# Six score bursts instead of five, six PSUM banks in strict turns, later stores and a reordered first chunk in a transformer block on one Trainium2 core

## The chip, the cores and the metric

The kernel runs as one program on one core of a Trainium2 chip. The metric is the device time of one execution in microseconds (us); smaller is better. A core has a matmul engine (TensorE, PE in the profile, with its weight loads on a row of their own, PEld), a vector engine (VectorE, DVE), an engine for activations (ScalarE, ACT), GpSimd (POOL) and a queue that only issues DMAs (SyncE, SP). Each engine runs its own instructions in the order of the program and waits on semaphores for the others.

## The reference

One input x of 2048 x 640 is normalised, and goes through an attention branch with a sliding window of 256 keys and through a gated feed-forward branch; both are added to x.

```python
def _A_ref(x, wqkv, wo):
    B, S, D = x.shape
    H = 32; Dh = D // H; W = 256
    qkv = (lambda x, *d: x.transpose(*d))((x @ wqkv).reshape(B, S, 3, H, Dh), 2, 0, 3, 1, 4)
    q, k, v = qkv[0], qkv[1], qkv[2]
    scores = jnp.einsum("bhqd,bhkd->bhqk", q, k) * (Dh ** -0.5)
    idx = jnp.arange(S)
    mask = (idx[:, None] - idx[None, :] >= 0) & (idx[:, None] - idx[None, :] < W)
    scores = jnp.where(mask[None, None], scores, -1e9)
    p = _softmax(scores, axis=-1)
    o = jnp.einsum("bhqk,bhkd->bhqd", p, v)
    return (lambda x, *d: x.transpose(*d))(o, 0, 2, 1, 3).reshape(B, S, D) @ wo

def _B_ref(x, w_gate, w_up, w_down):          # 640 -> 1728 -> 640
    g = jnp.einsum("bsd,df->bsf", x, w_gate)
    u = jnp.einsum("bsd,df->bsf", x, w_up)
    h = _gelu(g) * u
    return jnp.einsum("bsf,fd->bsd", h, w_down)

xn = _layernorm(x, axis=-1)
return x + _A_ref(xn, A_wqkv, A_wo) + _B_ref(xn, B_w_gate, B_w_up, B_w_down)
```

All tensors are float32.

## The kernel before, in words

**Precision.** A float32 product is made of three matmuls in a rounded format: the high part of one side by the high and the low part of the other, and low by high. The high part of a tile is a ScalarE copy (`xh`, `wqh`, `wvh`), the low part a subtraction on VectorE or GpSimd (`xl`, `wql`, `wvl`). A "dense group" (line 110) is 15 such matmuls (three times five pieces of 128 input features) into one PSUM tile of 512 tokens, `ps_d`, or of 320 v columns, `ps_v`.

**Chunks.** The 2048 tokens are four chunks of 512, each of four x tiles of 128 rows. A chunk is loaded (`ln_load`), normalised (`ln_stats`, `ln_sqrt`, `ln_rstd`; `ln_apply` is line 164, which scales the tile in place), turned by PE transposes through PSUM (`turn`, line 181, tiles `ps_t`) and split into xh and xl. The first chunk has a function of its own, `first_chunk`, whose order on PE, ScalarE, VectorE and GpSimd is written out by hand: x tiles 0 and 1 are the left half, tiles 2 and 3 the right half; `high(k)` (line 352) and `low(k)` (line 349) split one of five turned pieces; `high_qk` (line 361) and `low_qk` (line 366) split the weights of q (`w0`) and k (`w5`), and `part` is five matmuls of a half. A one-column GpSimd copy from an x tile (lines 378 and 397) serves only to hold the engine until that tile is scaled. `load_v` is a generator: its first step loads the v weights, five more split them (lines 301 and 302), and at its end `v_tiles` fills the v tiles' constant columns (lines 312 and 313). Outside the hand-written parts a scheduler at build time sets the order, so the fills of `ones` (lines 441 and 442, which eight DMAs then spread over the k tiles, line 445) and of `mask` (from line 467) stand wherever it finds a place on GpSimd.

**q and k.** `save_qk` takes a finished dense group of q or k apart into three bfloat16 layers of `pt` (two buffers): `upper` on ScalarE (line 277), `middle` on VectorE into the single buffer `r` (line 273), `lower` on ScalarE (line 258) and GpSimd (line 259), and `store`, DMAs by SP to DRAM (line 268). `load_stack` loads them back by SP in another layout (`ks<-kd`, `qs<-qd`, line 493).

**Attention.** There are 32 units (8 groups of four heads times four chunks), each of 14 slots. `defer(n, fn)` puts a step n slots later. In each slot PE gets what the hand-written order says and then dense matmuls as filler (`pull_fill`, 34.05 matmuls per unit). Three kinds of work use the ring of six PSUM banks, by `bank(name)`:

- `ps_m` (line 522), raw scores of which VectorE takes the row maximum (line 526, `mx`): four tiles in slot 0, four more behind the output in slot 0, four each in slots 4 and 8;
- `ps_e` (line 581), scores with the maximum folded in, of which ScalarE takes the exponential (line 583, `P`); a unit has twelve, and `SCORES` says in which slot each is made;
- `ps_o` (line 608), the product of the previous unit's P with v, copied out by ScalarE (`ob`, line 612); and `ps_n`, a small transpose of the maxima.

That makes 30 tiles a unit. GpSimd clears the masked corners of P (lines 594 and 597). `x_sums` makes sums of x tiles on GpSimd (`tx`, line 739) and stores them by SP (`td<-tx`, line 743).

`load_stack(u + 3)` stands in slot 9 of unit u for k and in slot 12 for q, so that SP's order is fixed by slots too.

**After attention** come the remaining gate and up products (line 952, 570 to 800 us), and then, in steps of `steps`, the down and output projections (line 1219). There each pass over 256 tokens has ten steps; a step n also prepares weights for later passes, as the table `plan` says. An operation `p20` stands for piece 0 of weight set t2, one ScalarE copy (line 1419) and one VectorE subtraction of the high part; `f` fetches, `h` and `l` split a whole set. At the end of a pass VectorE adds eight PSUM banks into the result (`drain`, with `u` and `m` as its scratch tiles).

Of the kernel before, what the change touches and what calls it, by code (L numbers as in the profile page):

```python
# [19 lines left out]
C = 512  # L20
# [11 lines left out]
BURSTS = 0, 4, 8  # L32
SCORES = {0: range(0, 1), 2: range(1, 5), 4: range(5, 7), 8: range(7, 9), 10: range(9, 12)}
RATE = 34.05
# [36 lines left out]
def block_kernel(ctx, tc, x, wqk, wv, wgu, wdo, wdl, out):  # L71
# [76 lines left out]
    def ln_sqrt(mv, n, lp):  # L148
        ve = lp.tile([128, n], F32, name="ve", tag="ve", bufs=2)
        sq = lp.tile([128, n], F32, name="sq", tag="sq", bufs=2)  # L150
        nc.vector.tensor_tensor(out=ve, in0=mv[:, :, 1], in1=eps[:, 0:n], op=OP.add)
        nc.scalar.activation(sq, mv[:, :, 1], AF.Sqrt, bias=eps[:, 0:1])
        return ve, sq
# [75 lines left out]
    def defer(n, fn, *a):  # L229
        if now[0] is None:  # L230
            fn(*a)
        else:
            at(now[0] + n, fn, *a)
# [17 lines left out]
    def save_qk(t, c, ps):  # L251
# [5 lines left out]
        def lower():  # L257
            nc.scalar.activation(pt[:, 1, :], r, AF.Copy)  # L258
            nc.gpsimd.tensor_tensor(out=pt[:, l, :], in0=r, in1=pt[:, 1, :], op=OP.subtract)  # L259
            defer(2, store)  # L260

# [71 lines left out]
    def run(*gens):  # L333
        for gen in gens:
            for _ in gen:
                pass
# [7 lines left out]

    def first_chunk(xs, wr0, wr5, lp):
        halves = slice(0, 256), slice(256, 512)
# [4 lines left out]
        def high(k, ps, cs):  # L351
            nc.scalar.activation(xh[:, k, cs], ps, AF.Copy)
# [6 lines left out]
        def high_qk(raw):  # L359
            wh = wp.tile([128, KT, 128], F32R, name="wqh", tag="wqh")  # L360
            nc.scalar.activation(wh, raw, AF.Copy)
            return wh
# [6 lines left out]
        with tc.manual_schedule(engines=MANUAL | {mybir.EngineType.Pool}):  # L369
# [13 lines left out]
            high(0, ta[0], halves[0])  # L383
            for k in range(1, 4):
                high(k, ta[k], halves[0])
            wh5 = high_qk(wr5)
            vb = ln_sqrt(mv[1], 2, lp)
            high(4, ta[4], halves[0])
            for k in range(2):
                low(k, ta[k], halves[0])  # L390
            rs = ln_rstd(*vb, 2, lp)
# [5 lines left out]
            nc.gpsimd.tensor_copy(one[:, 0:1], xs[3][:, 0:1])  # L397
            w5 = low_qk(wr5, wh5)
            tb = [turn(0, xs[2:4], "o")]
            for k in range(2, KT):  # L400
                low(k, ta[k], halves[0])
# [22 lines left out]
    with tc.tile_pool(name="lp", bufs=1, side="right") as lp:  # L424
# [11 lines left out]
        xs += [ln_load(t, lp) for t in range(4, 8)]  # L436
        w0, w5, mv1 = first_chunk(xs, wr0, wr5, lp)
        run(prep)
        v0 = v0[0]
        ones = lp.tile([4, 2 * C], BF, name="ones")  # L440
        nc.gpsimd.memset(ones, 0.0)
        nc.gpsimd.memset(ones[0:2], 1.0)
# [37 lines left out]
    pf.close()  # L480
    psr = pp.enter_context(tc.tile_pool(name="psr", bufs=6, space=PSUM, reuse_waits="tile"))
    ap = pr.enter_context(tc.tile_pool(name="ap", bufs=2, side="right", reuse_waits="tile"))

    def load_stack(u, which=(0, 1)):
# [4 lines left out]
        for i in which:  # L489
            dst, src, top, again = ((qs[u % NQ], qd[c], 1, 2), (ks[u % NK], kd[c], 0, 0))[i]  # L490
            for j in (0, 2):
                for p, part, n in ((j * 32, top, 2), (j * 32 + 2 * DH, again, 1), (64 - j * 32, 0, 3)):
                    nc.sync.dma_start(dst[p:p + DH * n, j:j + 2].rearrange("p j t -> p (j t)"),
                                      src[g, part:part + n].rearrange("s (d j) t -> (s d) (j t)",
                                                                      j=4)[:, j * C:(j + 2) * C])

    def bank(name):
        return psr.tile([128, C], F32, name=name, tag="ring")

# [228 lines left out]
    def x_sums(p, k, half):  # L728
# [12 lines left out]
        def store(i):  # L741
            t = live[i]
            defer(4, lambda: nc.sync.dma_start(td[p][i][:, k, half * w:half * w + w], t))

# [593 lines left out]
    for j, f in enumerate(range(NFA, NF - 1)):  # L1338
# [50 lines left out]
        if not end:  # L1389
# [14 lines left out]
            7: "ft6 ft8 hb8 lb8", 8: "ft7 ht6 lt6", 9: "ft0 ht8", 10: "lt8 ht7 lt7", 11: "ft1 ft2 ht0 lt0",  # L1404
            12: "ft3 ht1 lt1", 15: "p20", 17: "p21", 21: "p22", 22: "p23", 23: "p30", 24: "p31", 25: "p32", 26: "p33"}

# [101 lines left out]
```

## Time and profile before

| what | us |
|---|---|
| runs | 1047.75, 1049.51, 1049.57 |
| median | 1049.51 |
| the profiled execution's own time | 1048.57 |
| its span, first to last instruction | 1046.8 |
| PE busy in it | 1035.2 |
| VectorE, ScalarE, GpSimd busy | 730.8, 513.5, 333.8 |

The profile is that of one execution. Time of the profiled execution and span differ by what lies before the first and after the last instruction. In rows of the timeline the first column is the start, the second how long the instructions of the row lasted from the first start to the last end, then engine, line, operation, out<-in, and the count. What stands in square brackets is the engine's idle time ahead of the row and what ended it. In rows of waits the three numbers are the total, the number of waits and the longest. Ends of matmuls are modelled.

### The profile page before, as it was taken

How to read it: one execution, taken by the hardware profiler on the slowest of the kernel's cores; microseconds unless marked ns; L12 is line 12 of the kernel's file. 1: busy time of each engine (PE TensorE's matmuls, PEld its weight loads, DVE VectorE, ACT ScalarE, POOL GpSimd, SP SyncE). 2: the span in 40 equal slices, each digit the busy share in tenths (PEclk: the TensorE clock that was granted, in tenths of full speed). 3: DMA queues.
4: the chain of work that ended last, by engine and by line, in shares of the span. 5: the costliest groups of instructions: out<-in, count | busy, mean ns of one | idle time of the engine just before them, and what ended most of it. 6: DMA issues, size and time to landing. Idle time of an engine off the chain costs nothing.

```text
span 1046.8 us, 22733 instructions
## 1 busy us (share of the span) xinstructions
PE 1035.2 (99%) x7997; PEld 827.6 (79%) x7997; DVE 730.8 (70%) x2007; ACT 513.5 (49%) x1088; POOL 333.8 (32%) x503
## 2 busy tenths in 40 slices
PE   8999999999999999999999999999999999999998
PEld 7987666666677766666666888888888999999998
DVE  8745656666665556677662677877655889888887
ACT  4444666765665566656565532223324554333332
POOL 5122667766464458474635111110110000000000
PEclk9999999999999999999999999999999999999999
DMA  5651465545332344444322557677217874443342
GB/s 200 189 150 59 135 183 159 179 148 180 96 117 72 111 145 144 139 130 130 112 79 75 191 189 244 213 251 253 100 61 250 270 241 137 134 128 113 125 134 94
DMA packets 105179, 158.56 MB, mean 151 GB/s; under 512 B 15420, under 2 KB 60092, under 8 KB 105064
## 3 DMA queue, kind: packets, MB, share of 16 engines
q1 hardware_dynamic: 102680, 150.95, 45.0%
q10 hardware_dynamic: 2384, 6.16, 1.9%
q8 instruction: 63, 1.03, 0.4%
q14 instruction: 52, 0.43, 0.1%
HBM read 101.78 MB, written 54.92 MB: 150 GB/s over the span
## 4 chain that ended last, share of the span: by engine, by line
PE 92%; DVE 3%; DMA 2%; ACT 1%; POOL 1%; issue 1%; SPq 0%; DVEq 0%; POOLq 0%; ACTq 0%
PE ps_g L952 21%; PE ps L1219 21%; PE ps_d L110 21%; PE ps_e L581 8%; PE ps_o L608 7%; PE ps_v L110 7%; PE ps_m L522 4%; PE ps_g L110 1%; PE ps_t L181 1%; DVE junk L526 1%; DMA qs<-qd 1%; PE ps_d L356 1%; DVE ss L1057 0%; POOL pt L259 0%; DVE at L1057 0%
## 5 line engine op out<-in xcount | busy, mean ns | idle before, releaser
L526 DVE CUSTOM_DVE_ANT_0 junk<-ps_m,mask 128x320 bf16<-128x320 f32 (+2 forms) x512 | 243.2, 475 | 144.5 <-PE ps_m L522 85.5
L583 ACT ACTIVATE P<-ps_e 128x512 f32<-128x512 f32 (+2 forms) x384 | 195.6, 578 | 60.9 <-PE ps_e L581 59.0
L1219 PE MATMUL ps<-wb,at 128*128 128x320 f32 x999 | 156.0, 309 | 0.0
L1219 PEld LDWEIGHTS ps<-wb,at 128*128 128x128 f32 x999 | 148.9, 188 | 0.3
L594 POOL TENSOR_SCALAR_AFFINE_SELECT P<-P 128x512 f32<-128x512 f32 x128 | 83.9, 657 | 141.0 <-ACT P L583 138.3
L581 PE MATMUL ps_e<-qs,ks 124*128 124x128 bf16 (+2 forms) x704 | 108.0, 277 | 0.7 <-DVE mx L526 0.4
L110 PE MATMUL ps_d<-xh,wqh 128*128 128x512 f32 x350 | 104.4, 410 | 0.0
L110 PE MATMUL ps_d<-xl,wqh 128*128 128x512 f32 x350 | 104.2, 409 | 0.0
L110 PE MATMUL ps_d<-xh,wql 128*128 128x512 f32 x350 | 103.8, 409 | 0.0
L1219 PE MATMUL ps<-wt,at 128*128 128x320 f32 x552 | 89.2, 309 | 0.4 <-DVE u L1057 0.4
L581 PEld LDWEIGHTS <-ks 124*128 124x128 bf16 x704 | 50.8, 98 | 47.8 <-issue 30.1
L608 PE MATMUL ps_o<-P,v 128*32 128x384 f32 (+2 forms) x1408 | 84.3, 386 | 0.6 <-DVE mx L526 0.6
L1219 PEld LDWEIGHTS ps<-wt,at 128*128 128x128 f32 x552 | 82.9, 188 | 0.9 <-DVE u L1057 0.9
L597 POOL TENSOR_SCALAR_AFFINE_SELECT P<-P 128x512 f32<-128x512 f32 x112 | 70.8, 643 | 33.7 <-ACT P L583 33.7
L1173 ACT ACTIVATE at<-ss 128x512 fp32r<-128x512 f32 x59 | 37.3, 632 | 89.6 <-DVE ss L1057 89.6
L103 POOL TENSOR_TENSOR wql<-wr,wqh 128x640 fp32r<-128x640 f32 x11 | 17.6, 1607 | 174.0 <-PE ps_g L952 129.4
L110 PEld LDWEIGHTS ps_d<-xh,wql 128*128 128x128 f32 x350 | 63.9, 189 | 11.1 <-issue 0.3
L608 PEld LDWEIGHTS ps_o<-P,v 128*32 128x32 f32 x1408 | 41.5, 110 | 39.0 <-issue 21.1
L110 PEld LDWEIGHTS ps_d<-xl,wqh 128*128 128x128 f32 x350 | 63.8, 189 | 10.5 <-issue 0.2
L110 PEld LDWEIGHTS ps_d<-xh,wqh 128*128 128x128 f32 x350 | 63.4, 189 | 10.7 <-issue 0.3
L259 POOL TENSOR_TENSOR pt<-r,pt 128x512 bf16<-128x512 f32 x40 | 46.8, 1170 | 67.3 <-ACT pt L258 67.2
L612 ACT ACTIVATE ob<-ps_o 128x512 f32<-128x512 f32 x32 | 19.1, 597 | 86.6 <-PE ps_o L608 72.3
(194 smaller groups left out, 1846.0 us busy)
## 6 DMA issues: line engine op xcount, KB each, us to landing
hr<-hd SPq DMA_DIRECT2D x104, 128.0 KB
hd<-he SPq DMA_DIRECT2D x50, 256.0 KB
wr<-wgu SPq DMA_DIRECT2D x27, 320.0 KB
qs<-qd SPq DMA_DIRECT2D x64, 120.0 KB
ks<-kd SPq DMA_DIRECT2D x64, 120.0 KB
xi<-x SPq DMA_DIRECT2D x16, 320.0 KB
qs<-qd SPq DMA_DIRECT2D x64, 80.0 KB
ks<-kd SPq DMA_DIRECT2D x64, 80.0 KB
```

The lines of the kernel that those rows point to most:

```text
L110: nc.tensor.matmul(ps, a(k), b(k), start=n == 0, stop=n == 3 * nk - 1)
L259: nc.gpsimd.tensor_tensor(out=pt[:, l, :], in0=r, in1=pt[:, 1, :], op=OP.subtract)
L522: nc.tensor.matmul(ps[64 * h:64 * h + 64, lo:hi], q[rows, j, q0:q0 + 64], keys, start=True, stop=True, tile_position=(64 * r, 64 * h))
L526: nc.vector.tensor_tensor_reduce(out=junk[:, 0:n], in0=ps[:, 0:n], in1=mask[:, 320 - n:320], scale=1.0, scalar=NEG, op0=OP.add, op1=OP.max ...
L581: nc.tensor.matmul(ps[:, col:col + n], k[0:QROWS, j, kc:kc + 128], q[0:QROWS, j, q0:q0 + n], start=True, stop=True)
L583: nc.scalar.activation(pt[:, j, lo:hi], ps[:, lo:hi], AF.Exp, scale=SCALE)
L594: nc.gpsimd.affine_select(out=a, in_=a, pattern=[[0, 4], [1, 128]], compare_op=OP.is_ge, fill=0.0, base=0, channel_multiplier=-1)
L597: nc.gpsimd.affine_select(out=a, in_=a, pattern=[[0, 4], [-1, 128]], compare_op=OP.is_ge, fill=0.0, base=-1, channel_multiplier=1)
L608: nc.tensor.matmul(o[32 * j:32 * j + 32, q0:q0 + n], v[:, w0_:w0_ + 32], pt[:, j, col:col + n], start=i == 0, stop=i == len(todo) - 1, ski ...
L952: nc.tensor.matmul(ps, i, j, start=first and n == 0, stop=n == len(work) - 1, skip_group_check=True)
L1173: nc.scalar.activation(hi[:, 3:7], s, AF.Copy)
L1219: nc.tensor.matmul(ps[bank][:, 0:HD], *work[bank][j], start=bank not in begun, stop=final[p, bank] == n and j == len(work[bank]) - 1, skip ...
```

## The change

The diff does seven things.

1. `SCORES`: the twelve exponential scores of a unit are made in slots 0, 2, 4, 7, 8 and 10 as 1, 3, 2, 2, 2, 2, in place of 0, 2, 4, 8 and 10 as 1, 4, 2, 2, 3.
2. The store of `save_qk` is put four slots behind `lower` instead of two, and that of `x_sums` seven behind its last step instead of four.
3. The ring of six PSUM banks is no longer one pool with six buffers under one tag, but six tags with one buffer each, taken in turn.
4. `plan`: the pieces p20 to p33 come one or two steps earlier (p22 four).
5. In `first_chunk`, ScalarE makes the high part of the fifth piece, and the square root, ahead of the high part of the k weights; VectorE makes one low part instead of two ahead of the scaling of x tiles 2 and 3.
6. The split of the v weights and the fills of the v tiles are run inside `first_chunk`'s hand-written order, behind GpSimd's low part of the k weights, which stands behind x tile 3.
7. The fills of `ones` and `mask` get a one-column copy from x tile 3 ahead of them, so they too wait for that tile.

```diff
@@ -30,7 +30,7 @@
-SCORES = {0: range(0, 1), 2: range(1, 5), 4: range(5, 7), 8: range(7, 9), 10: range(9, 12)}
+SCORES = {0: range(0, 1), 2: range(1, 4), 4: range(4, 6), 7: range(6, 8), 8: range(8, 10), 10: range(10, 12)}
@@ -257,7 +257,7 @@
             nc.gpsimd.tensor_tensor(out=pt[:, l, :], in0=r, in1=pt[:, 1, :], op=OP.subtract)
-            defer(2, store)
+            defer(4, store)
@@ -342,7 +342,7 @@
-    def first_chunk(xs, wr0, wr5, lp):
+    def first_chunk(xs, wr0, wr5, lp, prep):
@@ -381,13 +381,11 @@
             high(0, ta[0], halves[0])
-            for k in range(1, 4):
+            for k in range(1, KT):
                 high(k, ta[k], halves[0])
+            vb = ln_sqrt(mv[1], 2, lp)
             wh5 = high_qk(wr5)
-            vb = ln_sqrt(mv[1], 2, lp)
-            high(4, ta[4], halves[0])
-            for k in range(2):
-                low(k, ta[k], halves[0])
+            low(0, ta[0], halves[0])
             rs = ln_rstd(*vb, 2, lp)
             ln_apply(xs[2], mv[1][:, 0, :], rs[:, 0:1])
             ln_apply(xs[3], mv[1][:, 1, :], rs[:, 1:2])
@@ -396,8 +394,9 @@
             nc.gpsimd.tensor_copy(one[:, 0:1], xs[3][:, 0:1])
             w5 = low_qk(wr5, wh5)
+            run(prep)
             tb = [turn(0, xs[2:4], "o")]
-            for k in range(2, KT):
+            for k in range(1, KT):
                 low(k, ta[k], halves[0])
@@ -434,10 +433,11 @@
-        w0, w5, mv1 = first_chunk(xs, wr0, wr5, lp)
-        run(prep)
+        w0, w5, mv1 = first_chunk(xs, wr0, wr5, lp, prep)
         v0 = v0[0]
         ones = lp.tile([4, 2 * C], BF, name="ones")
+        nc.gpsimd.tensor_copy(ones[:, 0:1], xs[3][0:4, 0:1])
+        nc.gpsimd.tensor_copy(mask[:, 0:1], xs[3][:, 0:1])
         nc.gpsimd.memset(ones, 0.0)
@@ -478,7 +478,7 @@
-    psr = pp.enter_context(tc.tile_pool(name="psr", bufs=6, space=PSUM, reuse_waits="tile"))
+    psr = pp.enter_context(tc.tile_pool(name="psr", bufs=1, space=PSUM, reuse_waits="tile"))
@@ -494,8 +494,11 @@
+    ring = [0]
+
     def bank(name):
-        return psr.tile([128, C], F32, name=name, tag="ring")
+        ring[0] += 1
+        return psr.tile([128, C], F32, name=name, tag=f"r{ring[0] % 6}")
@@ -740,7 +743,7 @@
-            defer(4, lambda: nc.sync.dma_start(td[p][i][:, k, half * w:half * w + w], t))
+            defer(7, lambda: nc.sync.dma_start(td[p][i][:, k, half * w:half * w + w], t))
@@ -1402,7 +1405,8 @@
-            12: "ft3 ht1 lt1", 15: "p20", 17: "p21", 21: "p22", 22: "p23", 23: "p30", 24: "p31", 25: "p32", 26: "p33"}
+            12: "ft3 ht1 lt1", 13: "p20", 15: "p21", 17: "p22",
+            21: "p23", 22: "p30", 23: "p31", 24: "p32", 25: "p33"}
```

## The prediction

> **What bounds the kernel now.** I read the page, then busy time by stage, then what the matmul engine (PE) waited for, then the timeline around those waits.
>
> ```profile
> PE 1035.2 (99%) x7997; PEld 827.6 (79%) x7997; DVE 730.8 (70%) x2007; ACT 513.5 (49%) x1088; POOL 333.8 (32%) x503
> ```
>
> ```profile
> 0.00:20.00 20.00, 15.57 (x142) 14.46 (x143) 15.61 (x50) 8.88 (x22) 12.78 (x31) 1.00 0.61 216
> ...
> 90.00:570.00 480.00, 476.67 (x4725) 319.42 (x4717) 298.93 (x1114) 297.77 (x648) 278.25 (x439) 1.00 0.42 128
> ...
> 1040.00:1046.80 6.80, 3.42 (x24) 3.16 (x22) 3.03 (x7) 0.00 (x0) 0.00 (x0) 0.89 0.22 81
> ```
>
> The columns are span, PE, weight loads, DVE, ACT, POOL, granted clock, DMA share, GB/s. PE is the bound: 1035.2 of 1046.8 us. The change takes no matmul away, so it can only move PE's idle time, 11.6 us: 4.4 in the first chunk, 3.3 in attention (90 to 570), 3.4 in the closing drain, which the diff does not touch, and 0.4 in the last stage. The clock is 1.00 throughout attention, so there is nothing to win there.
>
> ```profile
> PE ps_t L181 <- DVE xi L164: 2.4, 3, 1.5
> ...
> PE ps_d L356 <- ACT xh L352: 0.7, 1, 0.7
> PE ps_m L522 <- DVE r L273: 0.7, 1, 0.7
> PE ps_m L522 <- ACT ob L612: 0.7, 2, 0.3
> PE ps_m L522 <- DMA qs<-qd: 0.6, 1, 0.6
> PE ps_o L608 <- DVE mx L526: 0.6, 1, 0.6
> PE ps_e L581 <- DVE mx L526: 0.4, 2, 0.3
> PE ps L1219 <- DVE u L1057: 0.4, 1, 0.4
> ```
>
> Every part of the diff answers to one of these rows. The ends of matmuls are modelled, so a row shows less than is lost:
>
> ```profile
> 137.21 0.46 PE L522 MATMUL ps_m<-ks,qs 60*64 60x320 bf16 x5
> ...
> 138.00 0.33 PE L522 MATMUL ps_m<-ks,qs 60*64 60x320 bf16 x3 [0.33 <-ACT ob L612]
> ...
> 407.47 0.47 PE L522 MATMUL ps_m<-ks,qs 60*64 60x320 bf16 x8
> ```
>
> Eight such matmuls take 0.47 in one piece, but 138.33 - 137.21 = 1.12 here: 0.65 lost where 0.33 is shown. I put attention's 3.3 of shown idle at about 5 of loss.
>
> **First chunk.** Rows for the old order:
>
> ```profile
> 7.13 1.14 DVE L164 TENSOR_SCALAR xi<-xi,mv,rs 128x640 f32<-128x640 f32 x2
> ...
> 10.60 1.01 POOL L441 MEMSET ones<- 4x1024 bf16 x1
> ...
> 11.85 1.95 DVE L164 TENSOR_SCALAR xi<-xi,mv,rs 128x640 f32<-128x640 f32 x2
> 11.87 0.94 POOL L442 MEMSET ones<- 2x1024 bf16 x1
> 12.78 0.68 POOL L468 TENSOR_SCALAR_AFFINE_SELECT mask<-mask 128x320 f32<-128x320 f32 x1
> 13.22 0.33 PE L181 MATMUL ps_t<-ident,xi 128*128 128x128 f32 x1 [0.61 <-DVE xi L164]
> ...
> 14.91 1.72 POOL L302 TENSOR_TENSOR wvl<-wvall,wvh 128x320 fp32r<-128x320 f32 x2
> ...
> 21.77 1.17 POOL L259 TENSOR_TENSOR pt<-r,pt 128x512 bf16<-128x512 f32 x1 [1.80 <-ACT pt L258]
> ...
> 23.21 0.68 DVE L273 TENSOR_TENSOR r<-ps_d,pt 128x512 f32<-128x512 f32 x1
> ...
> 23.81 2.50 DVE L164 TENSOR_SCALAR xi<-xi,mv,rs 128x640 f32<-128x640 f32 x3
> ...
> 26.16 2.35 PE L181 MATMUL ps_t<-ident,xi 128*128 128x128 f32 x20
> ```
>
> Two applies (L164) take 1.14 at 7.13, where no GpSimd row stands beside them, and 1.95 beside the fills: 0.8 more, and PE's turn of tiles 2 and 3 waits for just these. Holding the fills back gives 0.8. Taking one of two `low` copies from ahead of the reciprocal gives another 0.3, and k = 4 of `high` ahead of the second weights ends the 0.7 wait for xh, but that PE time would run into the same turn, so it adds nothing. The applies then end at 11.85 + 1.95 - 0.8 - 0.3 = 12.7. The lows that move behind them cost DVE nothing before the turn, but within it the transposes wait for PSUM tiles that these lows free: I estimate 0.2. The first chunk ends some 0.9 earlier. PE then runs 40 v matmuls, to 26.16 in the old order, and meets the turn of tiles 4 to 7. That needs DVE's chain: statistics, `r` (L273), three applies. The old chain ends at 23.81 + 2.50 = 26.31, just as PE comes. The new one starts earlier only by what the moved lows leave, about 0.5, and `r` (one buffer) still waits for GpSimd's L259, which now queues behind wql, five wvl subtractions and the v fills. A wvl piece takes 1.72 / 2 = 0.86, wql is twice as wide (some 1.7), so from 12.7 that is 1.7 + 4.3 = 6.0, to 18.7, and the small v fills: before L259 is due near 21.77 - 0.5 = 21.3. But the ones and mask fills also look for a place there. So I keep 0.4 of the 0.9. Ends: 0.9 gained; 2.6 lost, if the fills (1.01 + 0.94 + 0.68 and two smaller) stand ahead of L259.
>
> Here a rule of the Trainium skill speaks against the change. The row is 1.95 against 1.14. The page SBUF — State Buffer, section "Who interferes with whom", says that VectorE in a two-port mode and GpSimd exclude each other for whole instructions. By it the moved work blocks the four applies of the next chunk instead, by up to one GpSimd instruction each: 4 x 1.17 = 4.7, of which three already pay 2.50 - 3 x 0.57 = 0.8, so that with the chain 0.5 earlier the sum below would end some 3 us higher, at 1049.4. The 2.50 beside L259 agrees with it in kind.
>
> **Attention.** Thirty tiles a unit in six PSUM banks; strict turns mean that each tile waits for the one six earlier. Both waits for `ob` and that of ps_o for a maximum can't be such (six back lie a maximum or an exponential long done), so they go: 2 x 0.65 + 0.6 = 1.9 gained. Score by score: slot 10's third score used to wait for the third maximum tile of slot 8; with two scores there only the first two count, and slot 2's fourth score, which waited for a maximum, is gone: the 0.4 shown, with what is hidden 1.0.
>
> The two waits for q (0.6 for the DMA, and 0.7 put down to `r`, where the row's load had just been issued) come from SP's queue:
>
> ```profile
> 402.39 0.81 SPq L268 DMA_DIRECT2D qd<-pt  x2
> 403.25 3.22 SPq L493 DMA_DIRECT2D ks<-kd  x6
> ...
> 407.01 2.22 SPq L493 DMA_DIRECT2D qs<-qd  x6
> ```
>
> SP stands at a store until GpSimd is done, and the loads behind it stand too. Two slots later for `save_qk` and three for the x sums put the store behind the k load in this unit; in the other the order stays, only a td store may move. I take 1.3 of about 1.7. The stores that pass behind a load land up to 3 us later; pt has two buffers, and most have more slack than that, so no price.
>
> Against this, a sixth burst of scores:
>
> ```profile
> 549.97 0.61 PE L581 MATMUL ps_e<-qs,ks 124*128 124x256 bf16 x4
> 550.28 0.53 PE L110 MATMUL ps_d<-xh,wql 128*128 128x512 f32 x1
> 550.65 1.09 PE L110 MATMUL ps_d<-xl,wqh 128*128 128x512 f32 x4
> 551.59 0.83 PE L581 MATMUL ps_e<-qs,ks 124*128 124x128 bf16 x6
> 552.12 0.54 PE L110 MATMUL ps_d<-xl,wqh 128*128 128x512 f32 x1
> 552.50 1.31 PE L110 MATMUL ps_d<-xh,wqh 128*128 128x512 f32 x5
> 553.64 1.07 PE L110 MATMUL ps_d<-xh,wql 128*128 128x512 f32 x4
> ```
>
> Dense matmuls come every 1.14 / 5 = 0.228. Burst and five dense take 551.59 - 549.97 = 1.62, so two score tiles cost 0.48; one tile more costs (552.12 - 551.59) - (550.28 - 549.97) = 0.22. A burst's fixed part is then 0.04, and 32 units pay 1.3. Ends: 0, and 4.5, if all of the 0.14 by which the first dense interval is longer (0.37) is lost.
>
> Slot 8's scores now take the banks of slot 7's, whose exponentials must be out:
>
> ```profile
> 235.63 0.61 PE L581 MATMUL ps_e<-qs,ks 124*128 124x256 bf16 x4
> ...
> 236.05 1.09 ACT L583 ACTIVATE P<-ps_e 128x512 f32<-128x512 f32 x2 [0.23 <-PE ps_e L581]
> 236.94 0.69 DVE L273 TENSOR_TENSOR r<-ps_d,pt 128x512 f32<-128x512 f32 x1 [2.32 <-POOL pt L259]
> ```
>
> Two scores are free 236.05 + 1.09 - 235.63 = 1.51 after the first began. PE reaches slot 8's second score after 0.48, 2.4 dense (0.55), four maximum tiles (0.47) and one score (0.22): 1.72. The margin is 0.2 with a free ACT. ACT runs 648 / 32 = 20 operations a unit, 14 of them exponentials, `ob` and the maxima's copy, so some six others fall on fourteen slots, and about 14 units have one in slot 7. One of 0.6 that starts with the slot holds the exponentials by 0.6 - 0.42 = 0.2, the margin itself; one that starts later by more. I take half of these units at 0.1: 0.7 (ends 0 and 8). Where DVE itself is late, as here (`r` waited 2.32 for GpSimd, and the maxima stand behind it), strict turns wait longer than a free choice of banks: 0.9 in two units, an estimate from that 2.32 less two slots. Attention: -1.9 - 1.0 - 1.3 + 1.3 + 0.7 + 0.9 = -1.3.
>
> **Last stage.** The p steps go one or two steps earlier.
>
> ```profile
> 890.90 0.48 DVE L1057 TENSOR_TENSOR wb<-stg,wb 128x320 fp32r<-128x320 f32 x1
> ```
>
> DVE sets the pace up to the drain for which PE waits 0.4; one of six subtractions (0.48) leaves that pass, so the wait with its hidden part goes: 0.5 (ends 0 and 0.7). The raw tiles are fetched earlier still.
>
> **Sum.** -0.4 - 1.3 - 0.5 = -2.2. The profiled execution took 1048.57 (span 1046.8, 1.8 around it), 0.9 under the median of three, 1049.51. 1048.57 - 2.2 = 1046.4.
>
> **Rivals.** *The waits change hands*: slot 7's burst at 2.5 in place of 1.3, q loads no earlier since SP's order around them stays, the first chunk's gain all spent at the next turn. Then -2.2 + 1.2 + 1.3 + 0.4 = +0.7 and 1049.3. For it: margins of 0.2, and a turn that DVE reached at 26.31. Against: `ob` and ps_o waits can't stay.
>
> *Slower, by ACT*: slot 8's second score waits for slot 7's second exponential. It decides at the 0.2 margin: with another ACT operation in slot 7 in half the units, 16 x 0.5 = 8, so +5.1 on the sum's side and 1053.7. For it: ACT is 62% busy in attention (297.77 of 480) and its order is fixed. Against: most of the six others start with their slot or lie elsewhere.
>
> *GpSimd's queue*: the fills stand ahead of L259; the turn of tiles 4 to 7 starts 2.6 late instead of 0.4 early: 1046.4 + 3.0 = 1049.4. For it: GpSimd was busy 12.78 of the first 20 us, and the work is held till 12.7. Against: the fills come later in the program. The page's rule above would end at the same place and shares this chance.
>
> **How the numbers follow.** A measurement of this kernel can tell about 0.2% (2.1 us) from no change; faster means below 1047.4. Forecast 0.44, all of it faster. Waits that change hands 0.24 and GpSimd's queue 0.13: mostly no change, of 0.37 together 0.34, with 0.03 slower. ACT 0.19, slower. So faster 0.44, same 0.34, slower 0.22. The forecast's own range is 1043.8 (all terms at their good ends but the drain) to 1047.4. The range over the cases is 1043.8 to 1052.0, which leaves out most of the ACT case and little below.
>
> **What would show it.** Right: the two applies at about 1.15, the turn of tiles 2 and 3 before 13.0, no PE wait for `ob`, none of ps_o for a maximum, idle in 90 to 570 under 2.5, no wait for `u`. Wrong: PE waits on ACT's P at slot 8, a PE gap near 26, a longer dense interval in every unit with idle unchanged.

## The result, and the profile after

| kernel | runs | median us | range | ratio to before [95%] |
|---|---|---|---|---|
| before | 6 | 1048.37 | 1047.64 to 1049.57 | |
| after | 6 | 1054.85 | 1053.43 to 1057.67 | 1.0062 [1.0047, 1.0077] |

The change made the kernel slower by 0.62%, some 6.5 us. Forecast was 1046.4, in a range that ended at 1052.0. The profiled execution of the changed kernel is its slowest run, 1057.67 (span 1055.9).

The page's busy times and the stages of the changed kernel, with the columns of the prediction's second fence:

```profile
PE 1041.0 (99%) x7997; PEld 827.3 (78%) x7997; DVE 728.1 (69%) x2007; ACT 516.5 (49%) x1088; POOL 333.4 (32%) x505
```

```profile
20.00:90.00 70.00, 68.50 (x443) 60.35 (x442) 42.48 (x122) 29.27 (x92) 18.29 (x21) 0.98 0.45 137
90.00:570.00 480.00, 473.60 (x4676) 313.90 (x4675) 297.64 (x1117) 294.48 (x641) 273.31 (x432) 1.00 0.43 127
...
24.75:28.16 3.41, 1.91 (x11) 1.08 (x10) 3.41 (x7) 0.72 (x5) 1.32 (x1) 1.00 0.48 136
28.16:31.57 3.41, 3.41 (x18) 3.41 (x17) 3.09 (x8) 2.50 (x5) 0.00 (x0) 0.50 0.36 115
157.87:161.28 3.41, 1.51 (x22) 0.91 (x21) 1.31 (x4) 1.37 (x4) 2.03 (x3) 1.00 0.59 156
161.28:164.69 3.41, 3.41 (x12) 2.01 (x10) 1.64 (x8) 1.03 (x4) 0.00 (x0) 0.50 0.44 131
```

The span grew by 9.1, PE's busy time by 5.8, though the matmuls are the same 7997. Twice the granted clock is 0.50 for 3.41 us (28.16 and 161.28), which adds 2 x 1.7 of "busy" time. The other 2.4 of it was not traced; ends of matmuls are modelled, so that a wait shows less idle time than it costs. The first half-clock window belongs to the start, the second to attention: the first score with the maximum folded in (`ps_e`) is made at 95.47 instead of 92.43, the last output (`ps_o`) at 579.75 instead of 570.51. So the start lost 3.0 (1.3 without its window) and from there to the last `ps_o` another 6.2 (4.5 without its window). The last stage, from its first `ps` to the last matmul, took 237.49 instead of 237.86.

What PE waited for:

```profile
PE ps_t L181 <- DVE xi L164: 3.1, 5, 1.5
PE ps_e L584 <- ACT P L586: 1.9, 5, 0.9
PE ps_m L525 <- DMA qs<-qd: 1.9, 2, 1.3
...
PE ps_e L584 <- DVE mx L529: 0.8, 3, 0.3
PE ps L1222 <- DVE u L1060: 0.4, 1, 0.4
```

Lines above 500 are three higher than before. The waits for `ob` and of `ps_o` for a maximum are gone. The wait of `ps_e` for P is new: slot 8's scores waiting for slot 7's exponentials, the mechanism that the prediction priced at 0.7 and its second rival at 8. One of the five, PE first, then ScalarE, in slots 7 and 8 of unit 4 (units are counted from 0, each from its first `ps_o` row to that of the next):

```profile
178.94 0.61 PE L584 MATMUL ps_e<-qs,ks 124*128 124x256 bf16 x4
...
180.16 0.47 PE L525 MATMUL ps_m<-ks,qs 60*64 60x320 bf16 x8
181.56 0.87 PE L584 MATMUL ps_e<-qs,ks 124*128 124x128 bf16 x4 [0.93 <-ACT P L586]
```

```profile
179.80 0.60 ACT L277 ACTIVATE pt<-ps_d 128x512 bf16<-128x512 f32 x1 [0.83 <-PE ps_e L584]
180.29 0.73 ACT L640 ACTIVATE wqh<-wr 128x640 fp32r<-128x640 f32 x1
180.92 2.14 ACT L586 ACTIVATE P<-ps_e 128x512 f32<-128x512 f32 x4
```

Slot 7's two scores stand ready after 178.94, but in ScalarE's order two other operations stand ahead of their exponentials, which start at 180.92; slot 8's scores, in the same two banks, follow the maxima of 180.16 by 1.40 instead of 0.4.

The start, GpSimd and VectorE, then SyncE, then PE:

```profile
19.35 0.94 POOL L441 MEMSET ones<- 4x1024 bf16 x1
...
21.99 0.45 POOL L470 TENSOR_SCALAR_AFFINE_SELECT mask<-mask 128x320 f32<-128x320 f32 x1
22.41 1.16 POOL L259 TENSOR_TENSOR pt<-r,pt 128x512 bf16<-128x512 f32 x1
```

```profile
11.46 1.14 DVE L164 TENSOR_SCALAR xi<-xi,mv,rs 128x640 f32<-128x640 f32 x2
...
23.61 0.69 DVE L273 TENSOR_TENSOR r<-ps_d,pt 128x512 f32<-128x512 f32 x1 [1.53 <-POOL pt L259]
24.22 0.15 DVE L160 SCALAR_TENSOR_TENSOR rs<-ve,rs 128x4 f32<-128x4 f32 x1
24.29 0.20 DVE L146 BATCH_NORM_AGGREGATE mv<-st 128x2 f32<-128x12 f32 x1
24.41 0.44 DVE L144 BATCH_NORM_STATS2 st<-xi 128x6 f32<-128x320 f32 x1
24.76 3.00 DVE L164 TENSOR_SCALAR xi<-xi,mv,rs 128x640 f32<-128x640 f32 x4
```

```profile
4.09 15.67 SPq L139 DMA_DIRECT2D xi<-x  x8
21.51 3.93 SPq L445 DMA_DIRECT2D ks<-ones  x6
```

```profile
12.13 0.33 PE L181 MATMUL ps_t<-ident,xi 128*128 128x128 f32 x1
...
26.77 0.33 PE L181 MATMUL ps_t<-ident,xi 128*128 128x128 f32 x1 [1.03 <-DVE xi L164]
...
27.82 3.61 PE L181 MATMUL ps_t<-ident,xi 128*128 128x128 f32 x17 [0.20 <-DVE xi L164]
```

The applies of tiles 2 and 3 take 1.14 and end at 12.60, and their turn starts at 12.13 instead of 13.22: the first gain is there. At the next turn (tiles 4 to 7) it is lost. The fills stand ahead of L259, and VectorE has the second `r`, the last reciprocal step and statistics of chunk 2 ahead of the four applies, where the old order had one apply ahead of the second `r`. The SyncE row shows where these statistics come from: the DMAs of `ones` wait for the held fills, so the loads of x tiles 8 to 11 now run ahead of them (eight loads in a row from 4.09). That this is why the scheduler at build time places their statistics early is argued, not shown: the two stand together in after, e1, e9 and e11, and neither is there in before, e4 and e8, but no run moved the loads alone.

### The profile page after: what moved, and what is told of

The parts are those of the page before. It is cut to its first block, busy times and chain, and to the rows that moved or that the text cites. A ratio compares the mean times of both kernels' runs of the same rounds, so it can differ in the third digit from the quotient of the medians.

```text
span 1055.9 us, 22725 instructions
## 1 busy us (share of the span) xinstructions
PE 1041.0 (99%) x7997; PEld 827.3 (78%) x7997; DVE 728.1 (69%) x2007; ACT 516.5 (49%) x1088; POOL 333.4 (32%) x505
## 3 DMA queue, kind: packets, MB, share of 16 engines
q8 instruction: 63, 1.03, 0.4%
## 4 chain that ended last, share of the span: by engine, by line
PE 89%; DVE 3%; ACT 2%; DMA 2%; POOL 2%; issue 1%; ACTq 0%; SPq 0%; DVEq 0%; POOLq 0%
PE ps_g L955 21%; PE ps L1222 21%; PE ps_d L110 20%; PE ps_e L584 8%; PE ps_o L611 7%; PE ps_v L110 6%; PE ps_m L525 4%; PE ps_g L110 1%; ACT P L586 1%; PE ps_t L181 1%; DMA qs<-qd 1%; DVE xi L164 0%; ACTq L549 0%; DVE ss L1060 0%; DMA wr<-wqk 0%
## 5 line engine op out<-in xcount | busy, mean ns | idle before, releaser
L586 ACT ACTIVATE P<-ps_e 128x512 f32<-128x512 f32 (+2 forms) x384 | 198.7, 574 | 63.7 <-PE ps_e L584 62.1
L584 PE MATMUL ps_e<-qs,ks 124*128 124x128 bf16 (+2 forms) x704 | 114.5, 278 | 4.0 <-ACT P L586 1.9
L110 PE MATMUL ps_d<-xh,wql 128*128 128x512 f32 x350 | 107.1, 415 | 0.0
L110 PE MATMUL ps_d<-xl,wqh 128*128 128x512 f32 x350 | 107.0, 414 | 0.0
L110 PE MATMUL ps_d<-xh,wqh 128*128 128x512 f32 x350 | 106.8, 414 | 0.0
L259 POOL TENSOR_TENSOR pt<-r,pt 128x512 bf16<-128x512 f32 x40 | 46.7, 1169 | 66.7 <-ACT pt L258 66.2
```

What stands on the lines that cost most here:

```text
L110: nc.tensor.matmul(ps, a(k), b(k), start=n == 0, stop=n == 3 * nk - 1)
L584: nc.tensor.matmul(ps[:, col:col + n], k[0:QROWS, j, kc:kc + 128], q[0:QROWS, j, q0:q0 + n], start=True, stop=True)
L586: nc.scalar.activation(pt[:, j, lo:hi], ps[:, lo:hi], AF.Exp, scale=SCALE)
```

## The experiments

Starts are those of the first `ps_e`; "attention" is from there to the start of the last `ps_o`, both in the one profiled execution of each run, which can differ from the median by up to 3 us. Each ratio is to the kernel before in the same set of runs; a point below is a percentage point of that ratio, some 10.5 us.

| run | median us | ratio [95%] | start | attention |
|---|---|---|---|---|
| before | 1048.37 | | 92.43 | 478.08 |
| after | 1054.85 | 1.0062 [1.0047, 1.0077] | 95.47 | 484.28 |
| e1, bursts as before | 1051.52 | 1.0038 [1.0023, 1.0052] | 93.91 | 478.72 |
| e2, first chunk as before | 1053.31 | 1.0052 [1.0037, 1.0067] | 92.45 | 481.85 |
| e3, both as before | 1051.15 | 1.0029 [1.0016, 1.0042] | 92.39 | 482.40 |
| e4, fills not held | 1052.25 | 1.0043 [1.0028, 1.0058] | 92.06 | 482.11 |
| e5, strict turns alone | 1049.88 | 1.0020 [1.0011, 1.0029] | 92.61 | 478.64 |
| e6, later stores alone | 1049.68 | 1.0011 [1.0001, 1.0020] | 92.65 | 478.36 |
| e7, six bursts alone | 1073.24 | 1.0235 [1.0221, 1.0249] | 92.60 | 501.84 |
| e8, first chunk without held fills, and plan | 1047.93 | 0.9991 [0.9982, 1.0000] | 92.14 | 478.09 |
| e9, sixth burst in slot 6 | 1051.59 | 1.0027 [1.0016, 1.0038] | 93.86 | 478.12 |
| e10, the same, fills not held | 1048.83 | 0.9999 [0.9990, 1.0008] | 92.18 | 478.15 |
| e11, as e8, fills behind tile 7 | 1049.04 | 1.0003 [0.9993, 1.0013] | 93.11 | 476.99 |
| e12, as e11, applies' order written out | 1046.95 | 0.9982 [0.9973, 0.9991] | 91.60 | 476.46 |
| e13, as e12, fills behind tile 3 | 1047.35 | 0.9992 [0.9983, 1.0001] | 91.94 | 479.42 |
| e14, the change, mended in both places | 1048.45 | 1.0001 [0.9992, 1.0010] | 91.63 | 478.37 |

**Parts of the change undone.** e1 puts back the five bursts, e2 the first chunk, e3 both; e4 leaves out only the two copies that hold the fills.

```diff
 e1, against after
-SCORES = {0: range(0, 1), 2: range(1, 4), 4: range(4, 6), 7: range(6, 8), 8: range(8, 10), 10: range(10, 12)}
+SCORES = {0: range(0, 1), 2: range(1, 5), 4: range(5, 7), 8: range(7, 9), 10: range(9, 12)}
```

> The changed kernel with the old five bursts of scores; first chunk, ring of banks, stores and plan stay changed. Theory: in attention the loss is slot 7's burst, whose two exponentials hold the banks that slot 8's scores need (some 5 us of waits for P in the trace after, and one window at half clock of 1.6). Then attention (first to last ps_o) takes 468 or less instead of 472.7, no wait of ps_e for P is left, and the time is 1049 to 1051. Rival: the strict turn of the six banks and the later stores cost it, whatever the bursts are: ps_e or ps_m still wait, attention stays at 471 to 473, and the time stays at 1053.5 to 1055.

1051.52, just above the theory's band, and no wait for P is left. Attention is 5.6 shorter, 3.9 of it besides the half-clock window that the other profile has. The rival falls. But the start is at 93.91, without any window: the first chunk by itself is 1.5 late.

```diff
 e2, against after (items 5 to 7 of the change undone)
-    def first_chunk(xs, wr0, wr5, lp, prep):
+    def first_chunk(xs, wr0, wr5, lp):
...
-        nc.gpsimd.tensor_copy(ones[:, 0:1], xs[3][0:4, 0:1])
-        nc.gpsimd.tensor_copy(mask[:, 0:1], xs[3][:, 0:1])
```

> The changed kernel with the first chunk of before; bursts, ring, stores and plan stay changed. Theory: the first chunk's part lost 3.0 in the profiled execution, of which 1.6 is the window at half clock that followed its gap; so first ps_e is back at 92.4, and the time is 1051.5 to 1053.5. Rival: the 3.0 is one profiled execution's mishap, and the first chunk as changed gains its 0.9 in most executions: then the time is 1055 to 1056.

1053.31, in the band, at its upper end: the start is back at 92.45, the waits for P stay (1.9, five times).

```diff
 e3, against before: items 2, 3 and 4 of the change alone
-            defer(2, store)
+            defer(4, store)
...
-        return psr.tile([128, C], F32, name=name, tag="ring")
+        ring[0] += 1
+        return psr.tile([128, C], F32, name=name, tag=f"r{ring[0] % 6}")
```

> Only ring of banks, stores and plan as changed; bursts and first chunk as before. Theory: the two parts that lost are out, and what is left is the waits for ob and for the maximum that strict turns take away, the earlier q loads and the last stage's 0.4: 1045 to 1047.5, under the kernel before. Rival: the strict turn costs as much as it gives where VectorE or ScalarE is late: 1048 to 1050.

1051.15: the theory falls, and the rival's 1048 to 1050 is too low as well. Turns, stores and plan, thought to gain, lose 0.29%. The profile has 2.2 of waits for `qs<-qd` and a window at half clock; the waits of `ps_e` for VectorE's maxima grew from 0.4 to 2.3.

```diff
 e4, against after
-        nc.gpsimd.tensor_copy(ones[:, 0:1], xs[3][0:4, 0:1])
-        nc.gpsimd.tensor_copy(mask[:, 0:1], xs[3][:, 0:1])
```

> The changed kernel, but the ones and mask fills are not held behind x tile 3 (the two gating copies are left out); the rest of the first chunk stays changed. Theory: the fills held back put GpSimd's subtraction for r 1.35 late and moved VectorE's applies of tiles 4 to 7 behind r; without it the turn of tiles 4 to 7 starts and ends as before (26.2 to 28.2), no half-clock window follows, the applies of tiles 2 and 3 are back at 1.95, and the time is 1051.5 to 1053. Rival: GpSimd's queue is full by the v weights moved ahead of the turn, with or without the fills: the turn stays late by 2 or more, and the time stays at 1054 to 1055.

1052.25: the theory. The start is 92.06, 0.37 better than before, and the next turn has no gap:

```profile
25.76 2.38 PE L181 MATMUL ps_t<-ident,xi 128*128 128x128 f32 x20
```

So what cost the start is the holding of the fills, not the v weights moved ahead of the turn. One point of the theory missed: the applies of tiles 2 and 3 take 1.67, not 1.95, and their turn starts at 12.58. Holding the fills was thus worth 0.45 there (12.13), and the new order of the rest 0.64 (12.58 against 13.22).

**Single parts on the kernel before.**

```diff
 e5, against before
-        return psr.tile([128, C], F32, name=name, tag="ring")
+        ring[0] += 1
+        return psr.tile([128, C], F32, name=name, tag=f"r{ring[0] % 6}")
```

> The kernel before with the strict turn of the six banks alone. Theory: strict turns are a loss where VectorE is late: with the first chunk and bursts of before, attention (first to last ps_o) grows from 465.7 by 1.3 to 2.5, in units 4, 8 and 17 above all (0.7, 1.3 and 0.6), with waits of ps_e for VectorE's maxima, and the two waits for ob go; time 1049 to 1050.5. Rival: the strict turn gains its 1.9 for ob and ps_o, and the loss of the run with both parts back came from the later stores: time 1045.5 to 1047.

1049.88, the theory. In PE's waits those for `ob` and of `ps_o` for a maximum are gone, and this row, 0.4 before, stands in their place:

```profile
PE ps_e L584 <- DVE mx L529: 2.0, 6, 0.7
```

```profile
236.93 0.69 DVE L273 TENSOR_TENSOR r<-ps_d,pt 128x512 f32<-128x512 f32 x1 [2.33 <-POOL pt L259]
```

```profile
238.07 0.38 PE L584 MATMUL ps_e<-qs,ks 124*128 124x128 bf16 x2 [0.71 <-DVE mx L529]
```

Here VectorE's `r` waits 2.33 for GpSimd, the maxima behind it are late, and the strict turn gives slot 10's scores the banks of just these maxima. This unit (8) is 1.25 longer than before, unit 4 0.69, 17 0.57, 0 0.45; units 2 and 9 are 0.65 shorter, unit 20 is 0.89 shorter. The profiled execution is only 0.8 over that of before, while the ratio gives 2.1 [1.2, 3.0], so the profile shows a part of the loss.

```diff
 e6, against before
-            defer(2, store)
+            defer(4, store)
...
-            defer(4, lambda: nc.sync.dma_start(td[p][i][:, k, half * w:half * w + w], t))
+            defer(7, lambda: nc.sync.dma_start(td[p][i][:, k, half * w:half * w + w], t))
```

> The kernel before with the later stores alone (q and k two slots, the x sums three). Theory: they take the waits for q of two units (0.9 in unit 20, and at 407) and cost nothing elsewhere: 1046.5 to 1048. Rival: the store moved ahead or behind the q load of unit 3 makes it late (2.2 of waits near 158 and a window at half clock in two profiles): attention 467.5 to 469 with the excess all in unit 3, time 1050 to 1051.5.

1049.68, between the two; by the interval it is 0.1 to 2.1 slower than before. Neither of the two waits for q is in its profile, and unit 20, where one of them was, is 0.88 shorter; but it is 0.89 shorter in e5 as well, with the stores of before. Units 5 and 9 are 0.64 and 0.55 longer, so that attention gains nothing. The last stage is 0.6 longer, in one wait (`ps` for `xr`, 0.4 shown). Why these places lose is open.

```diff
 e7, against before
-SCORES = {0: range(0, 1), 2: range(1, 5), 4: range(5, 7), 8: range(7, 9), 10: range(9, 12)}
+SCORES = {0: range(0, 1), 2: range(1, 4), 4: range(4, 6), 7: range(6, 8), 8: range(8, 10), 10: range(10, 12)}
```

> The kernel before with the six bursts of scores alone; banks chosen freely. Theory: the loss of the bursts (3.5 in attention) is that of slot 8's scores on slot 7's banks, which only a strict turn binds to the last two exponentials; with a free choice slot 8 finds a bank that is older, so attention grows by 1.0 to 1.5 at most (the sixth burst's price, 32 x 0.03 to 0.04), time 1048.5 to 1050. Rival: banks are all in use at slot 8 in any case, so the waits for P stay: attention grows by 3.5, time 1051 to 1052.

1073.24: neither. The loss is 25 us, and it is a wait for VectorE's maxima, which neither of the two expected:

```profile
PE ps_e L581 <- DVE mx L526: 19.8, 54, 0.6
```

```profile
337.80 0.47 PE L522 MATMUL ps_m<-ks,qs 60*64 60x320 bf16 x8
338.73 0.38 PE L581 MATMUL ps_e<-qs,ks 124*128 124x128 bf16 x2 [0.46 <-DVE mx L526]
339.37 0.38 PE L581 MATMUL ps_e<-qs,ks 124*128 124x128 bf16 x2 [0.27 <-DVE mx L526]
```

With a free choice, made at build time, slot 8's two scores got the banks of slot 8's own maxima in nearly every unit: 54 waits, two in each of 27 units, and a typical unit is 0.93 longer than before. So the price of the bursts depends on the banks: the bursts alone cost 24.6, strict turns alone 2.1, and both together, with the later stores, about 5 (e4: 4.5 in all, although its start and last stage are 0.7 shorter). The prediction priced the bursts under strict turns only; what each part does without the other is not in its sum.

```diff
 e8, against before: items 4, 5 and 6 of the change
+        w0, w5, mv1 = first_chunk(xs, wr0, wr5, lp, prep)
...
+            12: "ft3 ht1 lt1", 13: "p20", 15: "p21", 17: "p22",
+            21: "p23", 22: "p30", 23: "p31", 24: "p32", 25: "p33"}
```

> The kernel before with the first chunk's new order (ScalarE's and VectorE's parts of x, the v weights behind x tile 3), but the fills not held back, and with the new plan of the last stage; bursts, banks and stores of before. Theory: these are the two parts that gained, 0.37 at the first ps_e and 0.35 to 0.4 in the last stage: 0.7 less than the kernel before, about 0.05 to 0.1 per cent. Rival: the start's 0.37 is taken up by attention's own order, since it shifts nothing but time, or the last stage's is noise of single profiles (237.5 to 238.6 in five of them): then no difference.

1047.93, ratio 0.9991: the theory's size, at the edge of what can be told from no change. The start is 0.3 earlier, the last stage 237.58 instead of 237.86. SyncE here still issues `ones` ahead of x tiles 8 and 9:

```profile
12.28 5.16 SPq L443 DMA_DIRECT2D ks<-ones  x8
17.55 0.84 SPq L139 DMA_DIRECT2D xi<-x  x2
```

**The two losses, mended one by one.**

```diff
 e9, against after
-... 4: range(4, 6), 7: range(6, 8), 8: range(8, 10), ...
+... 4: range(4, 6), 6: range(6, 8), 8: range(8, 10), ...
```

> The changed kernel with the sixth burst in slot 6 instead of slot 7, all else as changed. Theory: slot 8's scores take the banks of the sixth burst's two exponentials, and from slot 6 these have one slot more (about 1.6 us), so the waits of ps_e for P go (1.9 shown, about 3.5 with what is hidden), attention is 467 to 468 besides any window at half clock, and the time is 1050.5 to 1052. Rival: what costs is a sixth burst as such, wherever it stands (the switch between the two kinds of matmuls, and DVE's late maxima under strict turns): attention stays at 470 to 471, time 1053.5 to 1055.

1051.59, 0.35 points under the change: the theory. No wait for P is left; in the same slot 8 as above the scores follow the maxima by 0.39:

```profile
175.96 0.47 PE L525 MATMUL ps_m<-ks,qs 60*64 60x320 bf16 x8
176.35 0.61 PE L584 MATMUL ps_e<-qs,ks 124*128 124x128 bf16 x4
```

The theory had slot 6's scores 1.6 earlier; by these rows and their own start (174.26) they are 1.70 ahead of the maxima, where slot 7's were 1.22 ahead, so 0.5. What changed is the order on ScalarE, where their exponentials (the second of them here) now stand ahead of the two other operations:

```profile
175.21 0.57 ACT L586 ACTIVATE P<-ps_e 128x512 f32<-128x512 f32 x1
175.76 0.60 ACT L277 ACTIVATE pt<-ps_d 128x512 bf16<-128x512 f32 x1
```

But the waits for VectorE's maxima, 0.8 in three places in after, are now these:

```profile
PE ps_e L584 <- DVE mx L529: 2.8, 9, 0.6
```

Attention is 478.12, no longer than with five bursts and strict turns (e1, 478.72); a sixth burst as such costs nothing that can be told (against before, the median difference of 31 unit lengths is -0.03). Four of the ten runs had a mean clock of 0.998 and took 1052.3 to 1053.8, the others 0.999 or 1.000 and 1049.8 to 1051.8. One window of 3.41 us at half clock would make 0.998; these runs have no profile, so that it comes and goes like this is an inference.

```diff
 e10, against e9
-        nc.gpsimd.tensor_copy(ones[:, 0:1], xs[3][0:4, 0:1])
-        nc.gpsimd.tensor_copy(mask[:, 0:1], xs[3][:, 0:1])
```

> The changed kernel with the sixth burst in slot 6 and the fills not held back. Theory: the two losses found (3.4 at the start and its window; 3.5 by exponentials) are both out; what is left of attention's loss is the strict turn where VectorE is late (1.2): 1048 to 1049.5, no different from the kernel before. Rival: the sixth burst costs anywhere: 1051.5 to 1052.5, as with the fills alone let free (1052.25).

1048.83, ratio 0.9999: the theory. With slot 6 for slot 7 (0.35 points) and the fills let go (0.28 points) the whole loss of 0.62 is accounted for. Each step is known to about 0.2 points. The step from slot 7 to slot 6 can be taken a second time, with the fills let go: e4 to e10, 0.44 points, and attention from 482.11 to 478.15.

```diff
 e11, against e8: the fills of ones (with their eight DMAs) and of mask behind x tile 7
+            if c == 1:
+                nc.gpsimd.tensor_copy(ones[:, 0:1], xs[7][0:4, 0:1])
+                nc.gpsimd.memset(ones, 0.0)
...
+                nc.gpsimd.tensor_copy(mask[:, 0:1], xs[7][:, 0:1])
```

> The kernel before with the first chunk's new order and the new plan, and the ones and mask fills held back until x tile 7 is scaled, behind GpSimd's subtraction for r (bursts, banks and stores of before). Theory: the start's loss was GpSimd's queue: with L259 back near 21.1, VectorE's r and the four applies come 1.3 earlier, the turn of tiles 4 to 7 waits for nothing, the 0.98 of the first turn stays: first ps_e 91.4 to 91.7, time 1.3 under the kernel before, 1046.5 to 1047.2. Rival: the start's loss is VectorE's order (the second r and the statistics of chunk 2 ahead of the four applies), which holding the fills back brings with it in any place: first ps_e 92.5 or more, time 1047.5 to 1049.

Start 93.11, 1049.04: the rival, whose band ended at 1049. L259 is on time (21.32), yet the applies come late:

```profile
21.49 1.02 DVE L159 SCALAR_TENSOR_TENSOR ve<-ve,rs 128x4 f32<-128x4 f32 x1
...
22.90 0.67 DVE L273 TENSOR_TENSOR r<-ps_d,pt 128x512 f32<-128x512 f32 x1
...
24.04 3.02 DVE L164 TENSOR_SCALAR xi<-xi,mv,rs 128x640 f32<-128x640 f32 x4
```

**VectorE's order written out.** e12 is e11 with the order fixed by hand; the statistics of tiles 8 to 11 are held by a small copy from tile 7 into their scratch tile.

```diff
 e12, against e11
+                    save_qk(0, 0, dn[0], lambda: vb.extend(ln_sqrt(mv, 4, lp)))
+                    rs = ln_rstd(*vb, 4, lp)
+            for j in range(4):
+                if j == 2:
+                    save_qk(5, 0, dn[1])
+                ln_apply(xs[4 + j], mv[:, j, :], rs[:, j:j + 1])
...
+            nc.vector.tensor_copy(st4[:, :, :, 0], hold[:, 0:8].rearrange("p (a b) -> p a b", b=2))
```

> As the run with the fills behind x tile 7, but VectorE's order there is written out: reciprocal and two applies of tiles 4 to 7, then the second r, then the other two applies, and the statistics of tiles 8 to 11 are held behind these applies. Theory: the start lost through two things, GpSimd's subtraction late by 1.3 and VectorE's statistics and second r ahead of the applies; with both out the turn of tiles 4 to 7 is entered near 25.3 and lasts 2.1, first ps_e 91.4 to 91.7, time 1.3 to 1.6 under the kernel before (1046.5 to 1047.2), no window at half clock. Rival: the 8 loads that the fills hold back, and the fills beside the applies of chunk 2, cost at the next turn what is gained here: first ps_e 92.3 or more, time 1047.5 to 1048.5.

1046.95, ratio 0.9982 [0.9973, 0.9991], start 91.60: the theory, and faster than both kernels.

```profile
21.05 2.00 DVE L164 TENSOR_SCALAR xi<-xi,mv,rs 128x640 f32<-128x640 f32 x2
22.98 0.68 DVE L280 TENSOR_TENSOR r<-ps_d,pt 128x512 f32<-128x512 f32 x1
23.58 1.12 DVE L164 TENSOR_SCALAR xi<-xi,mv,rs 128x640 f32<-128x640 f32 x2
24.74 1.02 DVE L171 COPY st<-xi 128x8 f32<-128x8 f32 x1
```

```profile
21.01 1.17 POOL L266 TENSOR_TENSOR pt<-r,pt 128x512 bf16<-128x512 f32 x1 [1.62 <-ACT pt L265]
24.40 1.32 POOL L266 TENSOR_TENSOR pt<-r,pt 128x512 bf16<-128x512 f32 x1 [2.22 <-ACT pt L265]
```

```profile
25.31 2.34 PE L188 MATMUL ps_t<-ident,xi 128*128 128x128 f32 x20
```

The last apply ends at 24.70, PE enters the turn at 25.31 and makes all 20 transposes without a stop.

```diff
 e13, against e12 (the fills of ones and mask back in their old place in the program)
+        nc.gpsimd.tensor_copy(ones[:, 0:1], xs[3][0:4, 0:1])
+        nc.gpsimd.tensor_copy(mask[:, 0:1], xs[3][:, 0:1])
...
-                nc.gpsimd.tensor_copy(ones[:, 0:1], xs[7][0:4, 0:1])
...
-                nc.gpsimd.tensor_copy(mask[:, 0:1], xs[7][:, 0:1])
```

> The same with the fills as in the changed kernel, behind x tile 3 and so ahead of GpSimd's subtraction for r (L259 of the change near 22.4). Theory: with VectorE's order written out only the second r waits for GpSimd (to 23.6), and the third and fourth applies stand behind it: they end near 25.5 to 25.9, so the turn loses 0.3 to 0.6, first ps_e 91.8 to 92.2, time 0.8 to 1.2 under the kernel before. Rival: GpSimd's queue alone makes the turn late whatever VectorE's order: first ps_e 93.5 or more as in the changed kernel without a window (93.9), time 1049 to 1050.

Start 91.94, the theory: with VectorE's order written out, GpSimd's queue costs 0.34 (91.94 against 91.60). VectorE's order by itself costs 1.5 (e11, 93.11 against 91.60), both together 2.3 (e1 and e9, 93.9); on top of the scheduler's order GpSimd's queue thus costs 0.8. 1047.35 is one tenth of a per cent over e12, within the intervals.

```diff
 e14, against after: e9's line, and the lines of e11 and e12
-... 4: range(4, 6), 7: range(6, 8), 8: range(8, 10), ...
+... 4: range(4, 6), 6: range(6, 8), 8: range(8, 10), ...
...
+                ln_apply(xs[4 + j], mv[:, j, :], rs[:, j:j + 1])
```

> The changed kernel mended in both places: sixth burst in slot 6, and the first chunk with the fills behind x tile 7 and VectorE's order written out; strict turns, stores and plan as changed. Theory: attention as with the sixth burst in slot 6 (466.4, 0.7 over before), start 0.9 under before, last stage 0.3 under: 1047 to 1048.2, just under the kernel before, and over the same start with the old bursts and free banks by 0.7. Rival: a start that is 0.9 earlier shifts the q loads of attention and brings waits for q back: 1049 or more.

1048.45, 0.25 above the theory's band, ratio 1.0001. Mended in both places, with burst 6 in slot 6 and e12's first chunk, the change is level with the kernel before; e12, with the old bursts, banks and stores and the same start, is 0.19 points better (2.0 us, where the theory had 0.7). So strict turns, bursts and stores together still lose. The row in which the two profiles differ most is that of the scores that wait for VectorE's maxima, e12 first, then e14:

```profile
PE ps_e L599 <- DVE mx L544: 0.4, 2, 0.3
```

```profile
PE ps_e L602 <- DVE mx L547: 3.0, 10, 0.5
```

## Why the prediction was wrong, point by point

The sum ended at -2.2, and +6.5 was measured. Three steps of it failed, all the same way. Slot 8 waiting for slot 7 was put at +0.7 and costs 3.7. The first chunk was put at -0.4 and costs some 2.6: 2.9 for the held fills (0.28 points, e9 against e10) less the 0.3 that the start gains without holding. Strict turns, q loads and the sixth burst as such were put at -2.0 together, and by e10 they come out near +0.4 (it is 0.1 faster than before, with a start that is 0.25 and a last stage that is some 0.3 shorter). Each of these measured sizes is known to some 2 us.

- **"It can only move PE's idle time."** Wrong in the profiled execution, where PE's busy time grew by 5.8: a gap can halve the clock afterwards, and that is counted as busy (3.4 of it).
- **First turn.** Right in kind: applies 1.14, turn 1.1 earlier. That the sum fits is luck: the forecast had 0.8 for the fills and 0.3 for the order, e4 gives 0.45 and 0.64. In e12 this gain lasts.
- **Next turn, "I keep 0.4 of the 0.9".** The step that failed in the start: 1.4 late instead of 0.4 early (e1 and e9, without the half-clock window). The third rival named GpSimd (L259 at 22.41, in e12 at 21.01), and its reason against, "the fills come later in the program", did not hold; but GpSimd is the smaller part (0.34 to 0.8 of 2.3). What the step left out is VectorE's order, 1.5 by e11 against e12: the applies stand behind the second `r` and behind statistics of chunk 2. Eight SyncE DMAs wait for `ones`, so x tiles 8 to 11 load early; that the statistics are early for this reason fits every profile, and no run isolates it. The rule of the Trainium skill, page SBUF — State Buffer, section "Who interferes with whom", agrees in kind: e12's two applies beside L266 take 2.00, the next two 1.12. Its price was 0.9 there, not the 4.7 that the prediction took as its bound (from which 4.7 - 0.8 - 0.5 makes 3.4, not 3.0), and the change did not raise it: the four applies of this turn are 1.7 over 4 x 0.57 in before (1.48 and 2.50) and 0.7 in after (3.00).
- **Waits for `ob` and `ps_o`, -1.9; slot 10 and slot 2, -1.0.** The rows for `ob` and of `ps_o` for a maximum vanish as forecast (after, e5). The row of `ps_e` for a maximum does not: 0.4 before, 0.8 in after, 2.0 in e5, 2.8 to 3.6 in e9, e10 and e14. Strict turns alone are 2.1 slower [1.2, 3.0] where -1.9 + 0.9 was forecast. The late VectorE, put at 0.9 in two units, is what the profiles show in place of the gain; that it makes up the whole of it is not shown.
- **q loads, -1.3.** Not shown. Unit 20, where one of the two waits was, is 0.87 to 0.94 shorter in all nine profiles with later stores, but also 0.89 in e5 with the old ones, and 0.51 to 0.67 in e8, e11 and e12. The waits listed for q come to 1.9 in after and 2.2 in e3 with later stores, none in e1; with the old stores none in e12 and 1.9 in e13. Their mean is 0.7 in the nine profiles with later stores and 0.6 in the seven with the old ones. What sets them was not found, and the stores alone gained no time (e6).
- **Sixth burst, +1.3.** Wrong: nothing that can be told (e9).
- **Slot 8 waiting for slot 7, +0.7.** The mechanism was right, the size was not: 3.7 (0.35 points, after against e9), and 4.6 in the second comparison (0.44 points, e4 against e10). The second rival, at 8 and 0.19, had the place and the cause, and twice the size. The "margin of 0.2" was missed where ScalarE had two operations ahead of the exponentials: in unit 4 they start at 180.92, 1.98 after the scores began, where the prediction had 0.42 and took a hold of 0.1 in half of 14 units. Instead five units waited, up to 0.9 each.
- **Last stage, -0.5.** About 0.3: eight of the nine profiles with the new plan and no other wait in this stage have 237.5 to 237.6, the ninth (e3) 237.8, before 237.86. But the wait for `u` of 0.4 stayed, so the reason was wrong, and where the 0.3 comes from is open.

Two of the prediction's three signs of being wrong came: PE waits on P at slot 8, and a gap near 26. The result lies outside the range because the misses add up, while the rivals were priced one at a time and the range left most of the ACT rival out.

## What to carry to other kernels

Where an operation is held back, follow everything that waits for its output, the DMA queue too: the smaller part of the cost here was the held work in GpSimd's queue (0.34 to 0.8), the larger the order that a scheduler made of VectorE's work (1.5), most likely after the loads that slipped ahead. A tile that takes the place of another in a bank inherits its reader's whole queue: before a burst is put one slot ahead of the user of its banks, list what that reader's engine has ahead of it. Two edits that act on the same ring must be costed together, since here one alone lost 24.6, the other 2.1, and both, with the later stores, about 5.

## What was not expected of the hardware

The clock was halved with no idle stretch of 3.41 us ahead of it: in the 3.41 us ahead of each half-clock stretch PE was busy for 1.91 and 1.51 (after) and for 1.26 (e3), and the longest idle pieces shown are 1.03, 1.26 and 1.50. The page TensorE: Matmul & The Clock Gate of the Trainium skill, section "What's actually happening", speaks of an idle window of about 3.4 us; here less was enough. The same gap of the start in e1's and e9's profiles, with 1.03 shown in its longest piece, had no half-clock stretch behind it. The same section calls the window free-running, and a gap that straddles two such windows would fit that, but no run here varied it.

A small VectorE operation beside GpSimd's subtraction took as long as what was left of it: the 128x8 copy of e12 1.02 (24.74 to 25.76, GpSimd until 25.72), the same copy in e13 1.02 (25.90 to 26.92, GpSimd until 26.88), and the 128x4 step of e11 1.02 (21.49 to 22.51, GpSimd until 22.49), where the same step took 0.14 in after.
